# Dividing the first evacuations between VectorE and ScalarE, and moving the second key and query transposes two units later

## The chip, the cores and the metric

One Trainium2 chip; the kernel runs on 1 of its cores. A core has TensorE (matrix products and transposes, writes to PSUM), VectorE, ScalarE, GpSimd, and queues that start DMA transfers, above all that of SyncE. The metric is device time in microseconds (us) of one execution. Three executions of the kernel before took 439.0, 439.33 and 446.64 us, median 439.33.

## The reference, cut to what matters

All in float32. Attention over 512 local and 32 global positions per head (4 batches, 8 heads, width 64), then a soft mixture of experts (8 experts with 4 slots each), then a dense layer with squared ReLU:

```python
def attention(q_l, k_l, v_l, q_g, k_g, v_g):
    out_g = softmax(scale * q_g @ concat(k_g, k_l).T) @ concat(v_g, v_l)
    s_ll  = where(abs(pos[:, None] - pos[None, :]) <= 32, scale * q_l @ k_l.T, -1e9)
    out_l = softmax(concat(scale * q_l @ k_g.T, s_ll)) @ concat(v_g, v_l)
    return concat(out_g, out_l)                   # 4 x 8 x 544 x 64 -> 2304 x 512 tokens
def moe(x):                                       # soft dispatch, 8 small MLPs, soft combine
    d = softmax(x @ phi, axis=tokens); c = softmax(x @ phi, axis=slots)
    return c @ experts(d.T @ x, w1, w2)
def dense(x):
    return maximum(x @ w_in, 0) ** 2 @ w_out
```

## The kernel before, in words

Attention comes first (about the first 155 us of the span), then the experts, then the dense layer. Only the first 60 us or so matter here.

**Units.** The local positions are cut into 16 blocks of 32. A unit is one block of queries and half of the heads: `("l", s, half)` has the local queries of block s, `("g", s, half)` the global queries against the keys that lie around block s. `units` lists 44 of them; their numbers go 0, 1 = `("l",0,0)`, `("l",0,1)`; 2, 3 = `("g",0,..)`; 4, 5 = `("l",1,..)`; 6, 7 = `("l",2,..)`; 8 = `("l",3,0)` and so on. "Unit 4" below is the fifth of them.

**What one unit runs through.** TensorE computes its scores (`emit_S`, L330 or L336) into one of two PSUM buffers. VectorE scans them in four pieces (L341: scale, mask, row minimum) into one `s_buf`. GpSimd subtracts the minimum (L354) from `s_buf` into `pe_buf`. ScalarE takes the exponential (`emit_exp`, L364). TensorE transposes the result (`emit_T`, L372, two PSUM buffers `pp`), VectorE or ScalarE copies it out (`PT_BY`; L144 is VectorE, L146 ScalarE). TensorE multiplies by the values (`emit_AV`, L391), VectorE divides by the row sum (L406 to L408).

**The order is written out by hand.** In step n of the main loop stand, in this order: scores of unit n, exponential of unit n-1, the items at place 0, value products of the units that are due (two units at a time, three steps later at the earliest), the transposes of unit n-2, the items at place 1, the items at place 2, then loads (`late`). Every engine works through its instructions in that order; a wait on one holds up all behind it.

**Items.** Keys and queries arrive in pairs of blocks, positions along the partitions, and must be transposed: `item_k(i, half)` and `item_q(s, half)` each issue four TensorE transposes (L219) into one of the two buffers of `ps_tr` and four copies (eight where the two blocks don't lie in order) from there into `kT` or `qz`. `K_AT` and `Q_AT` say in which step, at which place and by which engine. `load_k`, `load_q` and `load_v` bring the next pair or block; their issues stand in one row on SyncE's queue, and each waits until the buffer it fills has been read.

**The copies out of one PSUM tile.** Where VectorE and ScalarE both read the same PSUM tile, the program makes the second engine wait for the first.

**Before the loop.** `item_k(1)` (first pair of keys): half 0 copied by VectorE, half 1 by ScalarE. `item_q(0)` the same. `global_k`: heads 0 to 3 copied by ScalarE, heads 4 to 7 by VectorE. ScalarE needs one table load (L146, ACT_TABLE_LOAD) ahead of its first activation. Unit 0 needs the first half of each, unit 1 the second.

**What the change touches.** `item_k(3, 0)` and `item_k(3, 1)` stand in steps 0 and 1, `item_k(5, 0)` in step 5 ahead of the transposes of unit 3, `item_q(2, 0)` and `item_q(2, 1)` in steps 2 and 3. Unit 4 is the first that needs the keys of `item_k(3)`, unit 6 the first that needs the queries of `item_q(2)`, unit 8 the first that needs `item_k(5)`. Values: three blocks fit beside the global ones, so `load_v(s+3)` waits until the last value product of block s is done; the first such load waits for that of unit 3 and is needed by units 4 and 5.

## Time and profile before

| | |
|---|---|
| time, median of 3 executions | 439.33 us (439.0 to 446.64) |
| the profiled execution | 439.9 us, of it span 438.1 us (first to last instruction) |
| TensorE busy | 401.0 us, 92% of the span |
| VectorE, ScalarE, GpSimd busy | 295.7, 232.4 and 132.9 us |
| first scores (unit 0) begin | 12.90 us |
| value products of units 2 and 3 end, first later value load is issued | 31.64 and 31.71 us |
| value products of units 4 and 5 begin | 37.44 us |

How to read it: the page gives busy time by engine and the chain of work that ended last. The timeline lists instructions in order of time, runs of the same kind merged, each with its start, its duration and, in brackets, the idle time of its engine before it and what ended that. PE is TensorE, DVE VectorE, ACT ScalarE, POOL GpSimd, SPq the queue of SyncE.

### The profile page before, as it was taken

To read this page: it belongs to the slowest core of one execution; us is meant where nothing else is said; L and a number is where in the kernel's file an instruction comes from. 1 tells how busy PE (TensorE), PEld (TensorE's weight loads), DVE (VectorE), ACT (ScalarE), POOL (GpSimd) and SP (SyncE) were. 2 spreads that over 40 slices of the span, in tenths; PEclk is the share of its full clock that TensorE was granted. 3 is DMA by queue.
4 is the path that set the end of the run, shared out by engine and by line. 5 is a ranking of instruction groups with operands and counts; after the bars stand their busy time and mean duration, and the time that the engine had idled before them with its cause. 6 is when DMAs were issued, how large, how long until landed. Compare 5 with 4: busy or idle time off the path is not lost.

```text
span 438.1 us, 12444 instructions
## 1 busy us (share of the span) xinstructions
PE 401.0 (92%) x4899; PEld 305.6 (70%) x4899; DVE 295.7 (67%) x951; ACT 232.4 (53%) x539; POOL 132.9 (30%) x159
## 2 busy tenths in 40 slices
PE   6788879977988987998999999999999999999993
PEld 5676767765666764354587877878877888888882
DVE  5596877765897976212599999778996555644451
ACT  3677768787465332121467666565655443444441
POOL 6244543643444431110255533234542000000000
PEclk9899999999899899999999999999999999999997
DMA  5887987899273499999913434300002400500004
GB/s 144 203 248 197 290 258 191 305 259 329 68 244 110 113 368 360 356 406 408 392 56 106 128 105 120 119 3 0 1 1 50 95 1 12 132 3 1 0 0 121
DMA packets 54938, 69.03 MB, mean 158 GB/s; under 512 B 24032, under 2 KB 40416, under 8 KB 54880
## 3 DMA queue, kind: packets, MB, share of 16 engines
q1 hardware_dynamic: 53600, 67.45, 48.6%
q10 hardware_dynamic: 1280, 0.79, 0.6%
q8 instruction: 38, 0.62, 0.6%
q14 instruction: 20, 0.16, 0.1%
HBM read 63.77 MB, written 4.46 MB: 156 GB/s over the span
## 4 chain that ended last, share of the span: by engine, by line
PE 55%; DVE 19%; DMA 10%; issue 7%; ACT 5%; POOL 1%; SPq 1%; ACTq 1%; POOLq 0%; DVEq 0%
PE ops L1118 9%; PE ops L1119 9%; PE ops L1120 9%; DMA arena_v<-in_v_l_dram 4%; PE sp L330 3%; PE xp L391 3%; PE hps L913 3%; PE ops L941 3%; DVE arena_a L543 3%; DMA arena_a<-in_moe_w_out_dram 3%; PE pp L372 3%; DVE al L1090 3%; DVE arena_b L341 2%; DMA arena_b<-in_moe_w_in_dram 2%; PE hp L1079 2%
## 5 line engine op out<-in xcount | busy, mean ns | idle before, releaser
L1118 PE MATMUL ops<-w_hl,ah 128*128 128x512 f32 x272 | 107.6, 395 | 0.0
L1119 PE MATMUL ops<-w_hl,ah 128*128 128x512 f32 x272 | 106.7, 392 | 0.4 <-POOL w_hl L860 0.4
L1120 PE MATMUL ops<-w_hl,al 128*128 128x512 f32 x272 | 106.1, 390 | 0.0
L1083 DVE TENSOR_TENSOR arena_a<-hp,arena_a 128x384 f32<-128x384 f32 x96 | 46.8, 529 | 46.1 <-ACT arena_a L1082 46.0
L1082 ACT ACTIVATE arena_a<-hp 128x384 f32<-128x384 f32 x96 | 40.2, 471 | 66.0 <-PE hp L1079 65.9
L1120 PEld LDWEIGHTS ops<-w_hl,al 128*128 128x128 f32 x272 | 51.1, 188 | 11.3 <-DVE al L1090 0.3
L354 POOL TENSOR_TENSOR arena_r<-arena_b,nm 128x512 f32<-128x512 f32 x32 | 39.7, 1241 | 62.9 <-DVE nm L341 29.3
L1089 ACT ACTIVATE ah<-arena_a 128x384 fp32r<-128x384 f32 x96 | 45.0, 505 | 25.9 <-DVE arena_a L1083 25.9
L1118 PEld LDWEIGHTS ops<-w_hl,ah 128*128 128x128 f32 x272 | 51.0, 188 | 11.0 <-issue 0.8
L1119 PEld LDWEIGHTS ops<-w_hl,ah 128*128 128x128 f32 x272 | 51.1, 188 | 10.6 <-POOL w_hl L860 1.8
L1090 DVE TENSOR_TENSOR al<-arena_a,ah 128x384 fp32r<-128x384 f32 x96 | 50.0, 561 | 8.1 <-ACT ah L1089 4.1
L146 ACT ACTIVATE arena_b<-tp 64x256 f32<-64x256 f32 (+2 forms) x135 | 43.6, 350 | 12.6 <-PE tp L219 7.8
L558 POOL TENSOR_TENSOR arena_a<-arena_a 128x512 int32<-128x512 int32 x23 | 29.7, 1293 | 51.1 <-DVE arena_a L556 48.6
L330 PE MATMUL sp<-arena_b 64*32 64x128 f32 x1024 | 37.2, 283 | 5.3 <-issue 3.2
L341 DVE CUSTOM_DVE_ANT_0 arena_b<-sp,arena_r 128x128 f32<-128x128 f32 x128 | 29.5, 286 | 16.6 <-PE sp L330 10.9
L330 PEld LDWEIGHTS sp<-arena_b 64*32 64x32 f32 x1024 | 27.5, 110 | 12.8 <-issue 9.7
L364 ACT ACTIVATE arena_r<-arena_r 128x512 f32<-128x512 f32 x44 | 27.7, 629 | 15.4 <-POOL arena_r L354 15.1
L391 PE MATMUL xp<-arena_v,arena_t 128*32 128x65 f32 x1408 | 26.5, 223 | 9.0 <-ACT arena_t L146 3.6
L391 PEld LDWEIGHTS xp<-arena_v,arena_t 128*32 128x32 f32 x1408 | 21.9, 110 | 14.5 <-issue 4.6
L372 PE MATMUL pp<-ident,arena_r 128*128 128x128 f32 x176 | 29.3, 290 | 2.4 <-ACT arena_r L364 2.3
L860 POOL TENSOR_TENSOR w_hl<-arena_a,w_hl 128x512 fp32r<-128x512 f32 x16 | 21.4, 1338 | 32.2 <-DMA arena_a<-in_moe_w_out_dram 16.3
L372 PEld LDWEIGHTS pp<-ident,arena_r 128*128 128x128 f32 x176 | 19.1, 143 | 9.9 <-issue 3.8
(188 smaller groups left out, 591.0 us busy)
## 6 DMA issues: line engine op xcount, KB each, us to landing
arena_a<-in_moe_w_dram SPq DMA_DIRECT2D x35, 512.0 KB, 6.8
arena_b<-in_moe_w_dram SPq DMA_DIRECT2D x21, 512.0 KB, 7.3
arena_a<-in_moe_w_out_dram SPq DMA_DIRECT2D x16, 512.0 KB, 5.2
arena_v<-in_v_l_dram SPq DMA_DIRECT2D x16, 256.0 KB, 4.5
arena_b<-in_moe_w_in_dram SPq DMA_DIRECT2D x8, 512.0 KB, 4.9
arena_a<-in_moe_w_in_dram SPq DMA_DIRECT2D x8, 512.0 KB, 3.9
out_dram<-arena_a SPq DMA_DIRECT2D x64, 64.0 KB, 1.7
arena_k<-in_k_l_dram SPq DMA_DIRECT2D x30, 128.0 KB, 4.0
```

Source lines behind the costliest of these rows:

```text
L146: nc.scalar.activation(out=out, in_=in_, func=AF.Copy)
L330: nc.tensor.matmul(sp[r + 32 * e:r + 32 * e + 32, j], qz[d, (s + 2) % 3, hp, b], keys, start=True, stop=True, tile_position=(64 * e, r + 3 ...
L354: nc.gpsimd.tensor_tensor(out=pe.rearrange("p j (r k) -> p j k r", k=4), in0=s_buf.rearrange("p j (k r) -> p j k r", k=4), in1=nm.unsqueez ...
L372: nc.tensor.transpose(pp[:, j], pe_buf[n % NPE][:, j], ident)
L391: nc.tensor.matmul(xp[32 * b:32 * b + 32, 2 * h + e], p, V[:, b, 4 * half + 2 * h + e], start=True, stop=True)
L1082: nc.scalar.activation(out=r[:, :N], in_=hp[:, :N], func=AF.Relu)
L1083: nc.vector.tensor_tensor(out=a[:, :N], in0=hp[:, :N], in1=r[:, :N], op=ALU.mult)
L1089: nc.scalar.activation(out=ah[:, s], in_=a, func=AF.Copy)
L1090: nc.vector.tensor_tensor(out=al[:, s], in0=a, in1=ah[:, s].bitcast(F32), op=ALU.subtract)
L1118: nc.tensor.matmul(op, ah[:, s], w_hi, start=begin, stop=False)
L1119: nc.tensor.matmul(op, ah[:, s], w_lo, start=False, stop=False)
L1120: nc.tensor.matmul(op, al[:, s], w_hi, start=False, stop=end)
```

## The change

The copies of `item_k(1)`, `item_q(0)` and `global_k` are divided within each half: of each tile VectorE copies the first part (`e` = 0, or `i` = 0) and ScalarE the second. The copies of the global keys' heads 0 to 3 come ahead of those of the second half of the queries. Both engines have as many of these copies as before, 14 each. `item_k(3)` goes from steps 0 and 1 to steps 2 and 3, `item_q(2)` from steps 2 and 3 to steps 4 and 5, `item_k(5, 0)` from place 0 to place 2 of step 5, the loads that follow them likewise. The loads of the first two blocks of values and of the global values stand ahead of `load_q(2)` on SyncE's queue, and those of two of the four batches of global keys ahead of SyncE's part of `load_q(0)`.

```diff
@@ -221,11 +221,14 @@
 
     def global_k(kg_sb):
         tp = transpose4(kg_sb, ps_x, "x")
-        for n in range(2):
+
+        def evac_half(n):
             h = slice(2 * n, 2 * n + 2)
             for i in range(2):
                 evac(kT[:, h].rearrange("p h b s q -> p (h b) s q")[:, :, 6 + i, :],
-                     tp[:, h].rearrange("p h (b q) -> p (h b) q", b=B), 1 - n)
+                     tp[:, h].rearrange("p h (b q) -> p (h b) q", b=B), i)
+
+        return evac_half
 
     def global_q(qg_sb):
         tp = transpose4(qg_sb, ps_m, "m")
@@ -234,10 +237,12 @@
             evac(qgz.rearrange("p h b e q -> p (h b) e q")[s, :, e, :],
                  tp[s].rearrange("p h (b q) -> p (h b) q", b=B), e)
 
-    def item_k(i, half, who=1):
+    def item_k(i, half, who=1, other=None):
         tp = transpose_pairs(k_buf, half)
         p0, p1 = POS[i % 6], POS[(i + 1) % 6]
         for e in range(2):
+            if e and other is not None:
+                who = other
             for r in range(2):
                 src = tp[64 * r:64 * r + 64, e].rearrange("p h (b k q) -> p (h b) k q", b=B, k=2)
                 dst = kT[64 * e:64 * e + 64, 2 * half:2 * half + 2].rearrange("p h b s (q r) -> p (h b) s q r", r=2)[..., r]
@@ -247,11 +252,13 @@
                     evac(dst[:, :, p0, :], src[:, :, 0, :], who)
                     evac(dst[:, :, p1, :], src[:, :, 1, :], who)
 
-    def item_q(s, half, who=1, *where):
+    def item_q(s, half, who=1, *where, other=None):
         tp = transpose_pairs(q_buf, half, *where)
         z = qz[:, :, 2 * half:2 * half + 2].rearrange("p s h b (q r) -> p s (h b) q r", r=2)
         s0, s1 = (s + 2) % 3, s % 3
         for e in range(2):
+            if e and other is not None:
+                who = other
             for r in range(2):
                 src = tp[64 * r:64 * r + 64, e].rearrange("p h (b s q) -> p s (h b) q", s=2, q=16)
                 dst = z[64 * e:64 * e + 64, :, :, :, r]
@@ -289,11 +296,11 @@
     XT_BY = (0, 0, 0, 0, 0, 1, 0, 0, 0, 1, 0, 1, 0, 1, 1, 1)
 
     K_AT = {
-        1: (0, 0, 1), 2: (0, 2, 1), 3: (-1, 2, 1), 4: (0, 0, 1), 5: (-1, 2, 1), 6: (0, 2, 1), 7: (0, 2, 1),
+        1: (0, 2, 1), 2: (0, 2, 1), 3: (-1, 2, 1), 4: (0, 0, 1), 5: (-1, 2, 1), 6: (0, 2, 1), 7: (0, 2, 1),
         8: (0, 0, 1), 9: (-1, 2, 1), 10: (-1, 0, 1), 11: (0, 0, 0), 12: (-1, 2, 1),
     }
     Q_AT = {
-        0: (1, 1, 0), 1: (-1, 1, 0), 2: (0, 2, 1), 3: (0, 2, 1), 4: (-1, 0, 1), 5: (0, 1, 1), 6: (0, 0, 1),
+        0: (3, 1, 0), 1: (1, 1, 0), 2: (0, 2, 1), 3: (0, 2, 1), 4: (-1, 0, 1), 5: (0, 1, 1), 6: (0, 0, 1),
         7: (0, 2, 1), 8: (0, 0, 1), 9: (0, 2, 1), 10: (0, 1, 0), 11: (0, 0, 1), 12: (-1, 2, 1), 13: (0, 0, 0),
     }
 
@@ -620,10 +627,16 @@
         nc.vector.tensor_copy(out=perm.rearrange("p (b q) -> p b q", b=B), in_=ident.rearrange("p (q b) -> p b q", b=B))
         idle_products(7, ps_s, "s", ident)
         kg_sb, qg_sb = x_buf[0], x_buf[1]
+
+        def load_kg(b):
+            nc.sync.dma_start(out=kg_sb[32 * b:32 * b + 32], in_=k_g[b].rearrange("h q d -> q h d"))
+
         load_k(1)
+        load_kg(0)
+        load_kg(1)
         load_q(0)
-        for b in range(B):
-            nc.sync.dma_start(out=kg_sb[32 * b:32 * b + 32], in_=k_g[b].rearrange("h q d -> q h d"))
+        load_kg(2)
+        load_kg(3)
         for b in range(B):
             nc.sync.dma_start(out=qg_sb[32 * b:32 * b + 32], in_=q_g[b].rearrange("h q d -> q h d"))
         nc.vector.memset(V[:, :, :, D:VW], 1.0)
@@ -654,13 +667,13 @@
                 d, pos, who = Q_AT[s]
                 at(l0 if s % 2 else l1, pos, item_q, s + 1 if s % 2 else s + 2, s % 2, who, d=d)
             if s % 2 and s + 3 < NJ:
-                after(l0, load_q, s + 3)
+                after(l0 if s > 1 else l1, load_q, s + 3)
             if s % 2 == 0 and 0 < s <= NJ - 6:
                 after(l0, load_k, s + 5)
             at(l1, X_AT[s], emit_xT, s, d=av_at(index[l1]) - index[l1] + 1)
-        at(("l", 0, 0), 0, item_k, 3, 0, 1)
-        at(("l", 0, 1), 0, item_k, 3, 1, 1)
-        after(("l", 0, 1), load_k, 5)
+        at(("g", 0, 0), 0, item_k, 3, 0, 1)
+        at(("g", 0, 1), 0, item_k, 3, 1, 1)
+        after(("g", 0, 1), load_k, 5)
         for i in range(NM - 1):
             l1 = ("l", NT * i + NT - 1, 1)
             d = av_at(index[l1]) - index[l1]
@@ -696,10 +709,12 @@
                 fn(*args)
 
         for half in range(2):
-            item_k(1, half, half)
-        for half in range(2):
-            item_q(0, half, half, ps_pt, "pt")
-        global_k(kg_sb)
+            item_k(1, half, 0, other=1)
+        item_q(0, 0, 0, ps_pt, "pt", other=1)
+        evac_gk = global_k(kg_sb)
+        evac_gk(0)
+        item_q(0, 1, 0, ps_pt, "pt", other=1)
+        evac_gk(1)
 
         def load_vg():
             nc.sync.dma_start(out=V[3:128:4, :, :, 0:D].rearrange("p b h d -> p (b h) d"),
@@ -709,10 +724,10 @@
             nc.sync.dma_start(out=phi_sb, in_=phi.rearrange("(c p) s -> p c s", p=128))
 
         load_k(3)
-        load_q(2)
         load_v(1)
         load_v(2)
         load_vg()
+        load_q(2)
         late.setdefault(3, []).append((win_load, (0,)))
         late.setdefault(5, []).insert(0, (load_phi, ()))
         for n in range(NU + LA):
```

The program's order on ScalarE up to the last copy of the global keys (tp_193 and tp_202 are the halves of the first keys; tp_211 and tp_224, with the change tp_211 and tp_231, those of the queries; tp_237, with the change tp_224, the global keys), before, with the semaphores that each instruction waits for:

```order
L146 ACT_TABLE_LOAD
L146 ACTIVATE arena_b_91<-tp_202 64x8x2x16 [waits PE_49]
L146 ACTIVATE arena_b_91<-tp_202 64x8x2x16 x3
L146 ACTIVATE arena_b_91<-tp_224 64x128 [waits PE_49]
L146 ACTIVATE arena_b_91<-tp_224 64x128 x7
L146 ACTIVATE arena_b_91<-tp_237 128x8x32 [waits PE_49]
L146 ACTIVATE arena_b_91<-tp_237 128x8x32
```

and with the change:

```order
L146 ACT_TABLE_LOAD [waits DVE_49]
L146 ACTIVATE arena_b_91<-tp_193 64x8x2x16 [waits PE_49]
L146 ACTIVATE arena_b_91<-tp_193 64x8x2x16
L146 ACTIVATE arena_b_91<-tp_202 64x8x2x16 [waits DVE_49,PE_49]
L146 ACTIVATE arena_b_91<-tp_202 64x8x2x16
L146 ACTIVATE arena_b_91<-tp_211 64x128 [waits DVE_49,PE_49]
L146 ACTIVATE arena_b_91<-tp_211 64x128 x3
L146 ACTIVATE arena_b_91<-tp_224 128x8x32 [waits DVE_49]
L146 ACTIVATE arena_b_91<-tp_231 64x128 [waits DVE_49,PE_49]
L146 ACTIVATE arena_b_91<-tp_231 64x128 x3
L146 ACTIVATE arena_b_91<-tp_224 128x8x32 [waits DVE_49]
```

The first activation now reads a tile that VectorE reads first. Its wait for VectorE stands ahead of the table load, where before the table load waited for nothing.

ScalarE from there to the copy of the transposed exponentials of unit 1 (arena_r is `pe_buf`, pp the transposed tile, the tiles tp_287, tp_320, tp_336 and tp_376 those of `item_k(3)`), before:

```order
L146 ACTIVATE arena_b_91<-tp_287 64x8x2x16 [waits PE_49]
L146 ACTIVATE arena_b_91<-tp_287 64x8x2x16 x3
L364 ACTIVATE arena_r_99<-arena_r_99 128x512 [waits Pool_49]
L146 ACTIVATE arena_b_91<-tp_320 64x8x2x16 [waits PE_49]
L146 ACTIVATE arena_b_91<-tp_320 64x8x2x16 x3
L364 ACTIVATE arena_r_99<-arena_r_99 128x512 [waits Pool_49]
L146 ACTIVATE arena_t_79<-pp_358 128x512 [waits PE_49]
L364 ACTIVATE arena_r_99<-arena_r_99 128x512 [waits Pool_49]
L146 ACTIVATE arena_t_79<-pp_398 128x512 [waits PE_49]
```

and with the change:

```order
L371 ACTIVATE arena_r_99<-arena_r_99 128x512 [waits Pool_49] x2
L146 ACTIVATE arena_b_91<-tp_336 64x8x2x16 [waits PE_49]
L146 ACTIVATE arena_b_91<-tp_336 64x8x2x16 x3
L146 ACTIVATE arena_t_79<-pp_345 128x512 [waits PE_49]
L371 ACTIVATE arena_r_99<-arena_r_99 128x512 [waits Pool_49]
L146 ACTIVATE arena_b_91<-tp_376 64x8x2x16 [waits PE_49]
L146 ACTIVATE arena_b_91<-tp_376 64x8x2x16 x3
L146 ACTIVATE arena_t_79<-pp_385 128x512 [waits PE_49]
```

The copies of `item_k(3)` stood ahead of the exponentials of units 0 and 1; now they stand behind both, and ahead of the copies of the transposed tiles (arena_t) of units 0 and 1.

TensorE from the value products of units 0 and 1 to those of units 2 and 3 (sp are scores, xp value products, arena_k and arena_q the sources of the items' transposes), before:

```order
L391 MATMUL xp_438<-arena_v_95,arena_t_79 32x65 x16
L391 MATMUL xp_459<-arena_v_95,arena_t_79 32x65 x16
L372 MATMUL pp_480<-ident_64,arena_r_99 128x128 x4
L330 MATMUL sp_493<-arena_b_91 32x128 x16
L219 MATMUL tp_517<-arena_b_91,arena_k_83 128x128 x4
L372 MATMUL pp_530<-ident_64,arena_r_99 128x128 x4
L212 MATMUL tp_536<-ident_64,arena_a_75 128x128 x4
L330 MATMUL sp_546<-arena_b_91 32x128 x16
L391 MATMUL xp_570<-arena_v_95,arena_t_79 32x65 x16
L391 MATMUL xp_588<-arena_v_95,arena_t_79 32x65 x16
```

and with the change:

```order
L398 MATMUL xp_420<-arena_v_95,arena_t_79 32x65 x16
L398 MATMUL xp_441<-arena_v_95,arena_t_79 32x65 x16
L379 MATMUL pp_462<-ident_64,arena_r_99 128x128 x4
L219 MATMUL tp_468<-arena_b_91,arena_q_87 128x128 x4
L337 MATMUL sp_480<-arena_b_91 32x128 x16
L379 MATMUL pp_504<-ident_64,arena_r_99 128x128 x4
L219 MATMUL tp_510<-arena_b_91,arena_q_87 128x128 x4
L212 MATMUL tp_519<-ident_64,arena_a_75 128x128 x4
L219 MATMUL tp_525<-arena_b_91,arena_k_83 128x128 x4
L337 MATMUL sp_546<-arena_b_91 32x128 x16
L398 MATMUL xp_570<-arena_v_95,arena_t_79 32x65 x16
L398 MATMUL xp_588<-arena_v_95,arena_t_79 32x65 x16
```

Both halves of `item_q(2)` have come in (tp_468, tp_510), and `item_k(5, 0)` (tp_525) stands directly ahead of the scores of unit 6. `ps_tr` has two buffers, so tp_525 takes the one that tp_510 leaves, once VectorE has copied it. On VectorE the copies of tp_468 and one step of the w_in conversion (L553) stand ahead of the scans of unit 5, those of tp_510 directly behind them.

## Rows read from the trace of the kernel before

**Rows 1.** Page, part 5: xcount | busy us, mean ns | idle before.

```profile
L341 DVE CUSTOM_DVE_ANT_0 arena_b<-sp,arena_r 128x128 f32<-128x128 f32 x128 | 29.5, 286 | 16.6 <-PE sp L330 10.9
```

**Rows 2.** Stretches: length, busy us of PE, PEld, DVE, ACT, POOL; clock, DMA, GB/s.

```profile
12.90:23.60 10.70, 10.42 (x188) 8.29 (x188) 6.79 (x39) 6.79 (x14) 3.40 (x3) 0.84 0.84 204
23.60:31.70 8.10, 6.99 (x214) 5.42 (x210) 7.80 (x39) 5.39 (x15) 3.55 (x3) 1.00 0.89 261
...
160.00:180.00 20.00, 17.17 (x230) 8.69 (x234) 11.54 (x43) 3.66 (x16) 3.03 (x13) 1.00 0.94 338
```

**Rows 3.** Chain of waits, 33 to 46 us: start, us, what.

```profile
33.66 1.42 issue
...
37.51 1.08 PE xp L391 x64
...
38.65 5.74 DMA arena_v<-in_v_l_dram
...
44.52 1.14 PE xp L391 x64
```

**Rows 4.** Timeline to the first scores: start, us, engine, instruction, idle before.

```profile
3.74 1.28 ACT L146 ACT_TABLE_LOAD   x1 [3.74 <-issue]
...
7.52 1.73 DVE L144 COPY arena_b<-tp 64x256 f32<-64x256 f32 x4 [2.49 <-PE tp L219]
...
8.37 1.62 ACT L146 ACTIVATE arena_b<-tp 64x256 f32<-64x256 f32 x4 [3.35 <-PE tp L219]
...
8.73 1.61 PE L219 MATMUL tp<-arena_b,arena_q 128*128 128x128 f32 x8 [0.40 <-DMA arena_q<-in_q_l_dram]
...
10.38 2.47 ACT L146 ACTIVATE arena_b<-tp 64x128 f32<-64x128 f32 x10 [0.39 <-PE tp L219]
...
12.90 1.62 PE L330 MATMUL sp<-arena_b 64*32 64x128 f32 x32 [2.12 <-ACT arena_b L146]
```

**Rows 5.** Timeline, units 0 and 1, same columns.

```profile
15.36 1.06 PE L219 MATMUL tp<-arena_b,arena_k 128*128 128x128 f32 x4
...
18.60 0.63 ACT L364 ACTIVATE arena_r<-arena_r 128x512 f32<-128x512 f32 x1
...
18.76 1.14 POOL L354 TENSOR_TENSOR arena_r<-arena_b,nm 128x512 f32<-128x512 f32 x1 [1.87 <-DVE nm L341]
...
19.25 1.65 ACT L146 ACTIVATE arena_b<-tp 64x256 f32<-64x256 f32 x4
...
22.86 0.58 ACT L146 ACTIVATE arena_t<-pp 128x512 f32<-128x512 f32 x1
```

**Rows 6.** Timeline, units 2 to 6, same columns.

```profile
20.97 1.78 DVE L144 COPY arena_b<-tp 64x256 f32<-64x256 f32 x4
...
23.64 1.15 PE L391 MATMUL xp<-arena_v,arena_t 128*32 128x65 f32 x64
...
25.31 1.08 PE L330 MATMUL sp<-arena_b 64*32 64x128 f32 x32
...
25.68 0.29 DVE L341 CUSTOM_DVE_ANT_0 arena_b<-sp,arena_r 128x128 f32<-128x128 f32 x1
...
26.31 0.66 PE L219 MATMUL tp<-arena_b,arena_k 128*128 128x128 f32 x4
...
28.02 0.42 DVE L553 TENSOR_SCALAR arena_b<-arena_b 128x512 int32<-128x512 uint32 x1
...
30.97 0.67 PE L391 MATMUL xp<-arena_v,arena_t 128*32 128x65 f32 x32 [0.76 <-ACT arena_t L146]
```

**Rows 7.** Timeline, SyncE's queue: the key load behind item_k(3).

```profile
18.18 2.92 SPq L161 DMA_DIRECT2D arena_k<-in_k_l_dram  x4
```

**Rows 8.** DMA issues: KB, us to landing; w_in, values, global keys (4).

```profile
arena_b<-in_moe_w_in_dram SPq DMA_DIRECT2D x1, 512.0 KB, 4.7
...
arena_v<-in_v_l_dram SPq DMA_DIRECT2D x1, 256.0 KB, 5.1
...
DMA to landing us min/median/max: 3.1/3.9/4.8
```

## The prediction

> **What bounds the kernel now.** I read the stretches of busy time first, then the chain of waits in order of time, then the timeline of the first 45 us, because everything that the change touches lies there. The reader is to see three things. First, nothing is full in the beginning: the first scores start at 12.90 us, and TensorE had stood idle for 2.12 us, waiting for ScalarE's last copy [rows 4]. Second, between 23.60 and 31.70 us VectorE is the fullest engine, 7.80 of 8.10 us [rows 2]. Third, from there the chain runs through the values: the value products of units 4 and 5 start at 37.51, as soon as they are over the next block of values is requested (38.65), it lands 5.74 us later, and the products of units 6 and 7 start at 44.52, right behind it [rows 3]. So what counts for the end is not when the first scores start but when the products of unit 3 are done (30.97 + 0.67 = 31.64 [rows 6]), since the first later block of values is requested then and takes 5.1 us [rows 8]: it lands at 36.8, 0.7 before its use at 37.51. A delay beyond this 0.7 goes into the loads of values behind it.
>
> **The change, part by part.** The times of the kernel with the change that follow are estimates, from durations in the rows and the order in which the instructions now stand.
>
> *Division of the first copies.* The count is the same, 14 copies on each engine. Before, ScalarE loads its table at 3.74 for 1.28 us, in idle time, and starts copying at 8.37 [rows 4]. Now its wait for VectorE stands ahead of the table load. VectorE starts at 7.52 and needs 1.73 / 4 = 0.43 us a copy [rows 4], so two are done at 8.4. Then ScalarE loads until 9.7, copies four key pieces (1.62, to 11.4), four query pieces and one of the global keys. The 2.47 us for eight of the small kind and two of the large [rows 4] give 0.90 for the four and 0.33 for the one: 12.6. The first scores start at about 12.65 instead of 12.90. What the division gains, some 1.5 us, the table load takes back but for 0.25.
>
> *Loads in the beginning.* Two loads of global keys now stand ahead of two of the queries. The queries had landed when TensorE took them at 8.73, after a wait of 0.40 [rows 4]. What the queries lose is bounded by nothing from below and by the spread of the four loads of global keys from above (3.1 to 4.8 us to landing, so 1.7 [rows 8]). Without delay VectorE has copied its part of the first query half at 10.6, and ScalarE, with the keys until 11.4, hides 0.8 of it; the far end would leave 0.9. I take 0, which is nearer to a load of only 128 KB more in front. The values sooner on SyncE's queue are worth nothing: the first value products start at 23.64 behind TensorE's own work, with no wait for a transfer [rows 6]. `load_q(2)` behind them has until 26 us.
>
> *Second keys two units later.* Their transposes, 1.06 us [rows 5], and their copies no longer stand between the scores of units 0 and 1. With the 0.25 above, unit 1 is scanned about 1.1 us sooner, and GpSimd's subtraction for unit 1 ends at 18.8 instead of 18.76 + 1.14 = 19.9 [rows 5]. GpSimd reads the only `s_buf`, so the scans of units 2 and 3 come sooner as well, and without the query copies between them (1.78 us [rows 6]) unit 4 is scanned at 23.6 instead of 25.68 [rows 6].
>
> But ScalarE has the key copies behind both exponentials now. From 18.8 on it must do, in this order and without a pause: exponential 0.63, key copies 1.65, copy of the transposed unit 0 0.6, exponential 0.63, key copies 1.65, copy of unit 1 0.58 [rows 5]. That is 5.74, with the gaps between them 5.85: the copy for unit 1 is done at about 24.65, where it was done at 22.86 + 0.58 = 23.44 [rows 5]. The value products of unit 1 wait for it until 24.7; they end near 25.3 instead of 23.64 + 1.15 = 24.8 [rows 6]. All of TensorE's work stands behind them. So this part, 1.1 us ahead at first, is 0.5 us behind here.
>
> *Second queries two units later.* Behind these products TensorE transposes unit 2 and the first half of the queries, 0.6 each, to 26.4. VectorE then copies it (1.78), does a step of the w_in conversion (0.42 [rows 6]), scans unit 5 (4 x 29.5 / 128 = 0.9 [rows 1]) and copies the second half (1.78): 31.4. Only then is the PSUM buffer free for the transposes of `item_k(5, 0)`. Those take 0.66, the scores of unit 6 1.08, the products of units 2 and 3 1.15 [rows 6]: 34.2 to 34.5. Before, it was 31.64. The difference is 2.6 to 2.9; the 0.7 of slack leaves 1.9 to 2.2.
>
> *The loads that follow.* `load_k(5)` follows the moved transposes, 2.6 us later than at 18.18, and takes SyncE 2.92 us as before [rows 7]; the w_in block behind it is issued near 23.6 and lands 4.7 us later [rows 8], at 28.3, when VectorE asks for it: hidden, or 0.3 late. The load of `load_q(4)` now stands right ahead of the values that count, but is issued by 31.4.
>
> *Sum.* 1.9 to 2.2 us by the slack, up to 0.3 more for w_in: +2.2. Two things can move it. TensorE stood still for 1.42 us at 33.66 with no releaser in the profile [rows 3]; if that stop comes again behind the later scores of unit 7, the products of unit 4 start at 40.5 and not 39.7, +3.0. And in 12.90 to 23.60 the granted clock was 0.84 [rows 2], full speed and for a while half (1.2 instead of 2.4 GHz); without that drop the start would be some 0.5 to 1.3 us sooner, which leaves +0.9. The profiled execution took 439.9, so it would take 442.1; it stands 0.57 above the median of 439.33. Against the median: **441.5 us**, own range 440.2 to 442.4.
>
> **Rivals.**
>
> *The table load costs twice.* The trace shows the table load itself as 1.28 us [rows 4], and no instruction close behind it, so a further stop after it would not be seen in it. The Trainium skill (ScalarE: Activation LUTs, section "What ACT_TABLE_LOAD costs") puts a DRAIN of about 1.38 us beside a load of about 1.28, some 2.66 together; the load agrees with the trace, the drain no run here shows yet. As a mechanism of this kernel: if ScalarE stands still after the load for as long as the load takes, the first scores start at 13.9, the subtraction for unit 1 ends at 20.1 instead of 18.8, and all that follows comes 1.3 later: 442.8. Chance 0.08.
>
> *The delay is taken up.* Between 160 and 180 us DMA is busy 0.94 [rows 2]. If the weights for the experts come no later because attention runs later, the time is that of before, 439 to 440. For it: that share. Against it: the buffers into which these weights go come free only when attention is over. Chance 0.22.
>
> *The first gain is kept.* Unit 4 is scanned 2.1 us sooner (23.6 against 25.68 [rows 6]). If VectorE is the bound, as its 7.80 of 8.10 us say [rows 2], and the values are not, this gain goes through: 437.2. The point from which it decides: the products of unit 3 must end by 31.6 or sooner, so that the copies of the second queries and the transposes of `item_k(5, 0)` cannot follow one after the other as above. Against it: the order leaves no other way for the one PSUM buffer. Chance 0.26.
>
> *No difference in the order.* That the change doesn't do what it says is out: the order shows the moves.
>
> **How the numbers follow.** Forecast (slower by 0.9 to 3.1) 0.44, first gain kept 0.26, delay taken up 0.22, table load twice 0.08. The range leaves out the far end of the gain (sooner than 437.0, about 0.1) and of the delays (later than 443.2, about 0.08): 437.0 to 443.2. A difference of 2% is 8.8 us, about what a measurement of this kernel can tell from no change; none of the cases comes near it. For what none of them names I leave 0.02 on the fast side and 0.03 on the slow side: faster 0.02, within 2% 0.95, slower 0.03.
>
> **What the profile of the changed kernel would show.** Right: the table load near 8.4 and not 3.7; first scores near 12.65; the subtraction for unit 1 ending near 18.8; ScalarE without a pause from there to 24.65; the transposes of `item_k(5, 0)` near 31.5, waiting for VectorE; the value load behind unit 3 issued at 34.2 or later; the products of unit 4 near 39.7. Wrong: the table load early, or unit 3's products over before 32 us. The forecast as a whole is wrong if the products of unit 4 start 2 us later and the kernel still ends no later, or if unit 4 starts before 37.5.

## The result and the profile after

The kernel with the change takes 441.75 us, median of 22 executions (436.34 to 449.59). The kernel before was run as often beside it and has a median of 437.2 us (432.94 to 446.64). The ratio is **1.0078, 95% interval 1.0049 to 1.0107**: 3.4 us slower (2.1 to 4.7). The forecast of 441.5 us names the time to 0.3 us, but partly by luck: it stood on a median of 439.33 us from three executions and added 2.2 us, while 3.4 us were lost. A second set of the change, below, lost more (1.017), so the size of the loss is known only roughly. Ratios here and below compare undisturbed executions of both kernels, and the two profiled ones (443.9 us, span 442.1, of the change; 439.9 us, span 438.1, of before) are not among these.

**To the first scores** ([rows 4]): timeline of the kernel after, columns as there.

```profile
6.13 1.06 PE L219 MATMUL tp<-arena_b,arena_k 128*128 128x128 f32 x8 [1.43 <-DMA arena_k<-in_k_l_dram]
...
7.74 1.28 ACT L146 ACT_TABLE_LOAD   x1 [7.74 <-DVE arena_b L144]
9.03 1.62 ACT L146 ACTIVATE arena_b<-tp 64x256 f32<-64x256 f32 x4
9.04 1.08 PE L219 MATMUL tp<-arena_b,arena_q 128*128 128x128 f32 x4 [1.84 <-DMA arena_q<-in_q_l_dram]
...
10.16 1.45 DVE L144 COPY arena_b<-tp 64x128 f32<-64x128 f32 x5 [1.62 <-PE tp L219]
...
11.25 1.31 ACT L146 ACTIVATE arena_b<-tp 64x128 f32<-64x128 f32 x5 [0.60 <-DVE arena_b L144]
...
12.61 1.08 PE L337 MATMUL sp<-arena_b 64*32 64x128 f32 x32 [0.78 <-ACT arena_b L146]
```

The table load has moved from 3.74 to 7.74, and its releaser is VectorE. The first scores start at 12.61 (forecast 12.65). But ScalarE, which the forecast has working without a pause, waited 0.60 us at 11.25 for VectorE's query copies; these waited for TensorE, and TensorE had waited 1.84 us for the queries, where it waited 0.40 before. It took them only 0.31 us later than before (9.04 and 8.73); the wait is longer because the key transposes were over at 7.19 (6.13 + 1.06) instead of 8.33, as this line of before has it:

```profile
6.39 1.94 PE L219 MATMUL tp<-arena_b,arena_k 128*128 128x128 f32 x8 [1.70 <-DMA arena_k<-in_k_l_dram]
```

In this execution the table load was covered, and the queries set the time.

**Units 0 to 3** ([rows 5 to 7]): same view.

```profile
17.12 1.13 POOL L361 TENSOR_TENSOR arena_r<-arena_b,nm 128x512 f32<-128x512 f32 x1 [1.05 <-DVE nm L348]
18.28 0.63 ACT L371 ACTIVATE arena_r<-arena_r 128x512 f32<-128x512 f32 x1 [1.54 <-POOL arena_r L361]
...
18.94 1.64 ACT L146 ACTIVATE arena_b<-tp 64x256 f32<-64x256 f32 x4
...
21.62 1.61 ACT L146 ACTIVATE arena_b<-tp 64x256 f32<-64x256 f32 x4
...
23.26 0.60 ACT L146 ACTIVATE arena_t<-pp 128x512 f32<-128x512 f32 x1
...
23.91 0.67 PE L398 MATMUL xp<-arena_v,arena_t 128*32 128x65 f32 x32 [1.60 <-ACT arena_t L146]
...
25.64 1.79 DVE L144 COPY arena_b<-tp 64x256 f32<-64x256 f32 x4
...
28.07 0.43 DVE L560 TENSOR_SCALAR arena_b<-arena_b 128x512 int32<-128x512 uint32 x1 [0.65 <-DMA arena_b<-in_moe_w_in_dram]
...
29.36 1.78 DVE L144 COPY arena_b<-tp 64x256 f32<-64x256 f32 x4
...
31.24 0.63 PE L219 MATMUL tp<-arena_b,arena_k 128*128 128x128 f32 x4 [3.05 <-issue]
...
33.10 1.96 PE L398 MATMUL xp<-arena_v,arena_t 128*32 128x65 f32 x64
...
35.13 0.60 SPq L173 DMA_DIRECT2D arena_v<-in_v_l_dram  x1
```

This is the chain of the forecast, step by step: the subtraction for unit 1 ends at 18.25 instead of 19.9, ScalarE then has no pause until 23.86, unit 1's products wait 1.60 for it, VectorE copies the second queries from 25.64 to 27.43 and from 29.36 to 31.14, and only at 31.24 do the transposes of `item_k(5, 0)` run, behind a stop of 3.05 us. The profile names no releaser ("issue"); what ended right before is VectorE's copy. Unit 3's products end at 35.06, where they ended at 31.64.

The granted clock of stretches of the kernel after (length, busy us by engine, clock, DMA, GB/s):

```profile
11.96:32.45 20.49, 14.85 (x324) 11.54 (x328) 13.94 (x73) 11.81 (x30) 6.75 (x6) 1.00 0.76 190
32.45:35.86 3.41, 3.41 (x84) 2.85 (x77) 1.27 (x9) 2.66 (x9) 1.17 (x1) 0.50 0.74 261
...
169.00:179.20 10.20, 9.40 (x52) 4.11 (x48) 6.27 (x23) 0.93 (x4) 1.20 (x4) 0.50 0.70 278
```

1.2 us behind the end of the stop TensorE falls to 1.2 GHz for 3.41 us and is busy all of it. The products that took 1.15 us before take 1.96. The chain of waits ([rows 3]) goes on:

```profile
31.24 0.63 PE tp L219 x4
31.87 1.30 PE sp L337 x32
33.17 1.89 PE xp L398 x64
...
39.53 1.07 PE xp L398 x64
...
40.66 6.37 DMA arena_v<-in_v_l_dram
...
47.16 1.13 PE xp L398 x64
```

Units 4 and 5 come at 39.53 instead of 37.51, and TensorE works up to them without a wait for the values: the block issued at 35.13 landed 3.5 us later, where the one of before took 5.1. The next block takes 6.37 us instead of 5.74, and units 6 and 7 come at 47.16, 2.64 later than before.

When each later value load is issued (L173 on SyncE's queue, us from the start), in these two traces and in three of the experiments:

| | 1st | 2nd | 3rd | 4th | 5th | 6th | 7th | 8th | 9th | 10th | 11th | 12th | 13th | 14th |
|---|---|---|---|---|---|---|---|---|---|---|---|---|---|---|
| before | 31.7 | 38.6 | 45.7 | 56.5 | 65.0 | 72.0 | 83.8 | 91.3 | 98.0 | 115.8 | 122.3 | 129.2 | 142.4 | 149.8 |
| after | 35.1 | 40.7 | 48.3 | 58.4 | 67.9 | 74.6 | 86.5 | 94.3 | 101.3 | 115.8 | 121.8 | 131.7 | 144.0 | 150.1 |
| before again | 32.7 | 38.7 | 45.3 | 56.5 | 64.3 | 71.2 | 83.3 | 91.7 | 98.4 | 114.1 | 120.5 | 127.8 | 140.3 | 147.8 |
| value load later | 36.0 | 42.5 | 49.7 | 60.9 | 68.8 | 75.8 | 88.2 | 96.0 | 101.7 | 115.6 | 122.1 | 128.9 | 142.1 | 148.1 |
| division alone, table early | 31.1 | 37.1 | 43.8 | 54.8 | 64.5 | 71.1 | 82.7 | 90.7 | 97.9 | 112.2 | 118.1 | 125.1 | 138.3 | 144.3 |

Up to the ninth load the change is 1.9 to 3.4 us behind the first trace of before. At the tenth it is level: the trace of before has a stretch of half clock at 108.8 and another at 143.0, that of after at 93.9 and 128.0. The last load is 0.2 us late, and nearly all of the 4.0 us by which the two spans differ arises behind it, where the trace of the change has 10.24 us of half clock at 169. Against the second trace of before the change is 1.7 us late at the tenth load and 2.3 at the last. So this pair of traces shows how the delay arises, but not that it lasts. For that the experiments are needed.

The table shows a second loss. Between the 11th and the 12th load 10.0 us pass in the change, 6.9 and 7.2 in the traces of before. After, then before:

```profile
125.70 0.66 ACT L547 ACTIVATE arena_b<-arena_b 128x512 f32<-128x512 f32 x1 [4.53 <-DMA arena_b<-in_moe_w_in_dram]
...
126.94 0.66 PE L379 MATMUL pp<-ident,arena_r 128*128 128x128 f32 x4 [3.02 <-ACT arena_r L371]
```

```profile
124.69 0.67 ACT L540 ACTIVATE arena_b<-arena_b 128x512 f32<-128x512 f32 x1 [2.98 <-DMA arena_b<-in_moe_w_in_dram]
...
125.93 0.66 PE L372 MATMUL pp<-ident,arena_r 128*128 128x128 f32 x4 [1.50 <-ACT arena_r L364]
```

ScalarE must first convert a block of w_in that has not landed, and the exponential for which TensorE waits stands behind it. In seven of the fourteen traces (both of the change, moves alone, queries alone, both with the other PSUM pair, and the one with late second queries) this stop is 2.4 to 3.2 us long, half clock follows it or has already begun, and 9.3 to 10.2 us lie between the two loads; in the other seven the stop is 1.0 to 1.6 us long, there is no half clock, and 6.4 to 7.2 us lie between the loads. No experiment follows this up.

### The profile page after: what moved, and what is told of

It reads as the page before. It is cut to its first block, busy times and chain, and to the rows that moved or that the text cites. A ratio compares the mean times of both kernels' runs of the same rounds, so it can differ in the third digit from the quotient of the medians.

```text
span 442.1 us, 12447 instructions
## 1 busy us (share of the span) xinstructions
PE 404.5 (91%) x4899; PEld 307.7 (70%) x4899; DVE 294.8 (67%) x951; ACT 232.6 (53%) x539; POOL 132.6 (30%) x159
## 4 chain that ended last, share of the span: by engine, by line
PE 56%; DVE 14%; DMA 11%; ACT 7%; issue 6%; POOL 2%; SPq 2%; POOLq 0%; DVEq 0%; ACTq 0%
PE ops L1133 10%; PE ops L1134 9%; PE ops L1135 9%; DMA arena_a<-in_moe_w_out_dram 4%; PE sp L337 4%; PE hps L928 4%; PE xp L398 3%; PE ops L956 3%; PE pp L379 3%; ACT arena_b L146 3%; DMA arena_v<-in_v_l_dram 3%; PE hp L1094 2%; DMA arena_b<-in_moe_w_in_dram 2%; DVE arena_a L550 2%; DVE arena_a L563 2%
## 5 line engine op out<-in xcount | busy, mean ns | idle before, releaser
L146 ACT ACTIVATE arena_b<-tp 64x256 f32<-64x256 f32 (+1 forms) x135 | 43.6, 349 | 7.4 <-PE tp L219 4.1
L337 PE MATMUL sp<-arena_b 64*32 64x128 f32 x1024 | 36.3, 278 | 0.9 <-ACT arena_b L146 0.8
L398 PE MATMUL xp<-arena_v,arena_t 128*32 128x65 f32 x1408 | 28.3, 231 | 8.9 <-ACT arena_t L146 3.4
L398 PEld LDWEIGHTS xp<-arena_v,arena_t 128*32 128x32 f32 x1408 | 23.4, 116 | 14.9 <-issue 4.4
## 6 DMA issues: line engine op xcount, KB each, us to landing
arena_k<-in_k_l_dram SPq DMA_DIRECT2D x30, 128.0 KB, 4.0
```

The costliest lines, as they stand in the source:

```text
L146: nc.scalar.activation(out=out, in_=in_, func=AF.Copy)
L337: nc.tensor.matmul(sp[r + 32 * e:r + 32 * e + 32, j], qz[d, (s + 2) % 3, hp, b], keys, start=True, stop=True, tile_position=(64 * e, r + 3 ...
L398: nc.tensor.matmul(xp[32 * b:32 * b + 32, 2 * h + e], p, V[:, b, 4 * half + 2 * h + e], start=True, stop=True)
```

## The experiments

### Which part costs: division, moves, keys, queries

**Division alone** (the change with its moves undone, its load order kept):

```diff
 K_AT
-        1: (0, 2, 1),
+        1: (0, 0, 1),
 Q_AT
-        0: (3, 1, 0), 1: (1, 1, 0),
+        0: (1, 1, 0), 1: (-1, 1, 0),
...
-                after(l0 if s > 1 else l1, load_q, s + 3)
+                after(l0, load_q, s + 3)
...
-        at(("g", 0, 0), 0, item_k, 3, 0, 1)
-        at(("g", 0, 1), 0, item_k, 3, 1, 1)
-        after(("g", 0, 1), load_k, 5)
+        at(("l", 0, 0), 0, item_k, 3, 0, 1)
+        at(("l", 0, 1), 0, item_k, 3, 1, 1)
+        after(("l", 0, 1), load_k, 5)
```

> The change without its moves: the first copies divided, two loads of global keys and the value loads sooner, but the second key and query transposes where they stood before. Theory (the moves cost the time, the division costs nothing): first scores at 12.5 to 12.7 us, product of unit 3 over by 31.6, second value load requested near 38.7, ratio to the kernel before 0.998 to 1.001. Rival (the division, with the table load behind the wait for VectorE, costs the time): ratio 1.004 or more, as with the whole change, although the value products of units 4 and 5 are on time. A third outcome, the first scores 0.3 us sooner and this carried through, would be 0.999, which is not to be told from the theory.

Measured: ratio 1.0043 (0.997 to 1.0116), which holds both answers. In the trace the first scores start at 12.77, unit 3's products end at 32.19 (0.6 later than expected), units 4 and 5 start at 36.94, 0.5 sooner than in the first trace of before. Not settled by its time; by the trace the products of units 4 and 5 were on time.

**Moves alone** (the kernel before with the other side of that diff, loads and copies as before):

> The moves without the division: the first copies by whole halves as before, loads in the order of before, but the second key and query transposes two units later. Theory (the moves cost the time): first scores at 12.9 us, VectorE copies both halves of the queries between 25 and 31.5, the transposes of item_k(5, 0) at 31 to 32, value products of units 4 and 5 at 39 to 40, ratio to the kernel before 1.005 to 1.009. Rival (the division costs it): ratio 0.999 to 1.002, unit 4's products near 37.5.

Measured: ratio **1.0174 (1.0117 to 1.023)**, medians 442.29 and 436.98. First scores 12.84, and the same stop:

```profile
31.78 0.63 PE L219 MATMUL tp<-arena_b,arena_k 128*128 128x128 f32 x4 [2.43 <-issue]
...
33.35 1.13 PE L391 MATMUL xp<-arena_v,arena_t 128*32 128x65 f32 x64
...
39.84 1.13 PE L391 MATMUL xp<-arena_v,arena_t 128*32 128x65 f32 x64 [0.90 <-ACT arena_b L146]
```

The moves cost the time, more than the 1.005 to 1.009 expected, and more than the whole change in its first set (the intervals do not meet); sizes from different sets can therefore not be subtracted from each other. In this trace no half clock follows the stop, and units 4 and 5 wait for ScalarE and for the values, which landed 5.2 us after their issue at 34.55, until the same moment.

**The two moves apart**, each on the kernel before; queries (with the place of `item_k(5, 0)` and `load_q(4)`):

```diff
-        1: (0, 0, 1),
+        1: (0, 2, 1),
-        0: (1, 1, 0), 1: (-1, 1, 0),
+        0: (3, 1, 0), 1: (1, 1, 0),
-                after(l0, load_q, s + 3)
+                after(l0 if s > 1 else l1, load_q, s + 3)
```

> The kernel before with item_q(2) alone moved two steps later (with load_q(4) behind it and item_k(5, 0) at place 2 of step 5); the keys of item_k(3) stay where they were. By the prediction this is the larger part: transposes of item_k(5, 0) wait for VectorE's copy of the second half, unit 3's products end at 33.5 to 34.5 us instead of 31.6, units 4 and 5 start at 38.5 to 40, ratio 1.003 to 1.008. Rival (the keys behind both exponentials, which hold up ScalarE, are what costs): unit 3's products end before 32.2, ratio 0.998 to 1.002.

and keys:

```diff
-        at(("l", 0, 0), 0, item_k, 3, 0, 1)
-        at(("l", 0, 1), 0, item_k, 3, 1, 1)
-        after(("l", 0, 1), load_k, 5)
+        at(("g", 0, 0), 0, item_k, 3, 0, 1)
+        at(("g", 0, 1), 0, item_k, 3, 1, 1)
+        after(("g", 0, 1), load_k, 5)
```

> The kernel before with item_k(3) alone moved two steps later (with load_k(5) behind it); the queries of item_q(2) stay. By the prediction this is the smaller part, ScalarE's chain of two exponentials, two key copies and two copies of transposed tiles: unit 1's products end 0.5 us later than before, unit 3's products at 31.8 to 32.6, units 4 and 5 at 37.5 to 38.2, ratio 0.999 to 1.003. Rival (this is the larger part): unit 3's products after 33.5, ratio 1.004 or more.

Measured: queries 1.0108 (1.0041 to 1.0174), keys 1.005 (1.0007 to 1.0094). The trace of the queries alone, then of the keys alone:

```profile
32.38 1.09 PE L219 MATMUL tp<-arena_b,arena_k 128*128 128x128 f32 x4 [2.43 <-issue]
35.26 1.96 PE L391 MATMUL xp<-arena_v,arena_t 128*32 128x65 f32 x64
...
41.50 1.14 PE L391 MATMUL xp<-arena_v,arena_t 128*32 128x65 f32 x64
```

```profile
27.93 0.63 PE L219 MATMUL tp<-arena_b,arena_k 128*128 128x128 f32 x4 [1.56 <-DMA arena_k<-in_k_l_dram]
...
32.73 0.67 PE L391 MATMUL xp<-arena_v,arena_t 128*32 128x65 f32 x32 [1.69 <-ACT arena_t L146]
...
37.64 1.14 PE L391 MATMUL xp<-arena_v,arena_t 128*32 128x65 f32 x64 [0.17 <-DMA arena_v<-in_v_l_dram]
```

The queries are the larger part: unit 3's products end at 37.22 (half clock from 31.0 for 6.83 us), 2.7 us past the far end of what was expected, and units 4 and 5 come 4.1 us late. The keys alone end unit 3's products at 33.40, beyond the expected 32.6, by a wait not foreseen: their load moves with them, and `item_k(5, 0)` at its old place waits 1.56 for it. But the value load had nearly that much slack, since it landed 4.0 us after its issue: units 4 and 5 are 0.2 late against the first trace of before (1.0 against the second, below). The ratios agree in order; their intervals overlap.

### The first scores: table load or queries

**The change with its table loaded early:**

```diff
         load_q(0)
+        nc.scalar.activation(out=slots[:, 0, 0:1], in_=ident[:, 0:1], func=AF.Copy)
         load_kg(2)
```

> The whole change, and one tiny ScalarE activation ahead of the first copies (one column of the identity into the column of slots that the kernel writes later), so that the table is loaded in idle time, near 3.7 us. The prediction's own step (the table load takes back 1.2 us of the division's gain): first scores near 11.4 us, ScalarE's first key copies at about 7.7. Theory from the trace of the change (ScalarE waits for VectorE's query copies anyway, TensorE for the queries): first scores at 12.3 to 12.6. Time: equal to the whole change within 0.002 by both, since the later copies of the queries bind.

Measured: ratio 1.0131 (1.0066 to 1.0196), not clear of the change's 1.0078. Table load at 3.74, key copies from 8.31, then

```profile
9.29 1.09 PE L219 MATMUL tp<-arena_b,arena_q 128*128 128x128 f32 x4 [1.11 <-DMA arena_q<-in_q_l_dram]
...
11.50 1.30 ACT L146 ACTIVATE arena_b<-tp 64x128 f32<-64x128 f32 x5 [1.50 <-DVE arena_b L144]
...
12.85 1.93 PE L337 MATMUL sp<-arena_b 64*32 64x128 f32 x32 [0.77 <-ACT arena_b L146]
```

The early load buys nothing: ScalarE only waits longer, 1.50 instead of 0.60, and the first scores come even a little later than expected, with the queries. That the table load alone holds them back, which would give 11.4 here, is refuted.

**Division without moves, table early, queries ahead of all global keys:**

```diff
         load_k(1)
-        load_kg(0)
-        load_kg(1)
         load_q(0)
+        load_kg(0)
+        load_kg(1)
         load_kg(2)
         load_kg(3)
+        nc.scalar.activation(out=slots[:, 0, 0:1], in_=ident[:, 0:1], func=AF.Copy)
```

> The division without the moves, with the queries loaded ahead of all global keys as before the change, and one tiny ScalarE activation ahead of the first copies, so that the table is loaded near 3.7 us. Theory (with the division the queries' landing sets the first scores, and TensorE's pause for them keeps it at half clock): queries transposed right behind the keys at 8.3 to 8.8, the 64x128 score products of unit 0 from 11.2 to 11.9 us, ratio to the kernel before 0.994 to 1.000. Rival (the copies themselves or the clock set the first scores): first scores at 12.4 or later, ratio as for e1_divide_only.

Measured: ratio 1.0009 (0.9959 to 1.0058). First scores at 12.10, later than 11.2 to 11.9: the query transposes came at 8.53 without a wait, but the first four took 1.09 us, where the next four took 0.60. With both limits gone, 0.8 us are gained on the kernel before. They are lost again at 21.48, where the loads of values stand ahead of `load_q(2)` and the second queries, not moved here, are late:

```profile
21.48 1.08 PE L219 MATMUL tp<-arena_b,arena_q 128*128 128x128 f32 x4 [2.89 <-DMA arena_q<-in_q_l_dram]
```

**The same with `load_q(2)` ahead of the values, as before the change:**

```diff
         load_k(3)
+        load_q(2)
         load_v(1)
         load_v(2)
         load_vg()
-        load_q(2)
```

> The division alone, in the load order of the kernel before (queries ahead of all global keys, second queries ahead of the values), with the table loaded early and no moves: the version that by the experiments so far has only the gain of the division. Theory: first scores at 11.9 to 12.2 us (12.10 with this start in e7_divide_queries_first) instead of 12.90, no wait for the second queries, unit 3's products over by 30.8 to 31.6, ratio 0.996 to 1.000. Rival (nothing of the beginning's gain reaches the values): unit 3's products at 31.6 or later, ratio 1.000 to 1.002.

Measured: ratio 0.994 (0.989 to 0.999), medians 437.52 and 440.08. First scores at 12.19, unit 3's products over at 31.01, units 4 and 5 at 35.95. **The kernel before once more**, beside it on the chip:

> The kernel before once more, unaltered, as a measure of what two sets of runs of one kernel differ by, and for a second trace of it: ratio 0.997 to 1.003. The stretches of half clock (at 13.3, 108.8 and 143.0 us in the first trace) fall elsewhere if they belong to the execution and not to the kernel; the products of unit 3 should be over near 31.6 and units 4 and 5 start near 37.5 again.

Measured: ratio 0.9959 (0.9898 to 1.002), median 440.35. Unit 3's products end at 32.62, 1.0 us later than in the first trace, and units 4 and 5 start at 36.61, 0.8 sooner; differences of this size between two traces are not an effect of an edit. Half clock stands at 14.2 and 140.5 us, near two of the three places of the first trace; that at 108.8 does not come again. Two sets of one kernel can thus differ by 0.4%, and the version with the division alone is not shown to be faster than before: it is 2.6 to 2.8 us below both medians, and in the table its value loads are between 0.2 us behind and 3.5 us ahead of the second trace of before. Shown is that the division, with loads and table in the right place, costs nothing.

### The stop: buffer, queue or transfers

**The change, the second half of `item_q(2)` transposed into the other PSUM pair**, so that `item_k(5, 0)` needs not wait for VectorE:

```diff
-                at(l0 if s % 2 else l1, pos, item_q, ..., s % 2, who, d=d)
+                at(l0 if s % 2 else l1, pos, item_q, ..., s % 2, who, *((ps_pt, "pt") if s == 1 else ()), d=d)
```

> The whole change, but the second half of the queries of item_q(2) is transposed into the other PSUM pair (ps_pt), so that item_k(5, 0) needs not wait until VectorE has copied it out. TensorE's order stays that of the change. Theory (the wait for this one buffer is the step that costs the time): transposes of item_k(5, 0) near 28.2 us instead of 31.2, product of unit 3 over by 31.5 to 33, units 4 and 5 at 37.5 to 38.2, ratio to the kernel before 0.999 to 1.003. Rival (ScalarE's chain behind both exponentials, or the late w_in block, costs the time): value products of units 4 and 5 still after 39, ratio 1.006 or more.

Measured: ratio 1.0184 (1.0136 to 1.0233), medians 443.44 and 436.98.

```profile
29.54 0.60 PE L219 MATMUL tp<-arena_b,arena_k 128*128 128x128 f32 x4
30.07 1.08 PE L337 MATMUL sp<-arena_b 64*32 64x128 f32 x32
31.07 1.13 PE L398 MATMUL xp<-arena_v,arena_t 128*32 128x65 f32 x64
...
39.35 1.14 PE L398 MATMUL xp<-arena_v,arena_t 128*32 128x65 f32 x64 [2.63 <-DMA arena_v<-in_v_l_dram]
```

```profile
29.29 3.04 SPq L161 DMA_DIRECT2D arena_q<-in_q_l_dram  x4
32.37 1.07 SPq L603 DMA_DIRECT2D arena_a<-in_moe_w_dram  x2
33.54 0.60 SPq L173 DMA_DIRECT2D arena_v<-in_v_l_dram  x1
```

The stop is gone and unit 3's products end at 32.20, as expected. But `load_q(4)`, which moved with the queries, and two loads of weights behind it hold SyncE's queue until 33.5, and the values come at 39.35: a stop of 2.63 in place of the one removed (no half clock follows it). So the numbers of the rival came true, though not by the waits it named. The theory as stated, that the wait for the buffer is the cost, fails: it is only the first of several limits.

**The same, the two loads of weights behind the value load:**

```diff
     PIECES = (
-        0, 0, 0, 0, 1, 2, 0, 0, 1, 1, 1, 1, ...
+        0, 0, 0, 0, 1, 0, 2, 0, 1, 1, 1, 1, ...
```

> The kernel of e4_q2h1_pt, with the two loads of expert weights that stood ahead of the first later value load on SyncE's queue put behind it. In e4 unit 3's products were over at 32.2 us, but the value load was issued only at 33.54, behind load_q(4) and these two, and landed at 39.3. Theory (with the PSUM buffer free, SyncE's queue is what is late next): value load issued at 32.3 to 32.6, landing 5.1 to 5.8 later, products of units 4 and 5 at 37.4 to 38.4, the weights 2 us later at no cost, ratio to the kernel before 1.000 to 1.004. Rival (the landing time is set by how much the other loads move, not by the order of issue): units 4 and 5 still after 39.

Measured: ratio 1.0158 (1.0094 to 1.0222), medians 445.68 and 439.02, on a second chip.

```profile
35.23 0.67 PE L398 MATMUL xp<-arena_v,arena_t 128*32 128x65 f32 x32 [0.17 <-DMA arena_v<-in_v_l_dram]
...
44.27 1.57 PE L398 MATMUL xp<-arena_v,arena_t 128*32 128x65 f32 x64 [2.64 <-DMA arena_v<-in_v_l_dram]
```

The value load is issued at 30.75 and units 4 and 5 start at 35.23, 2.2 us sooner than before. The next value load, issued at 37.15 behind the weights, lets units 6 and 7 start at 44.27, as before the change, behind a stop of 2.64. "At no cost" was wrong. With the stop gone and units 4 and 5 ahead of before, the kernel is still as slow as the change itself on that chip (1.017, below): nothing of the loss is shown to come back. Why it ends 1.6% later though level with the one before at 44 us is open; its trace has half clock at 44.8, 92.6, 126.7 and 143.8, and 10.0 us between the 11th and the 12th value load, as the change has.

### Does a delay of the values reach the end?

The kernel before, the first later value load behind the key load of its step:

```diff
             late.setdefault(av_at(last_of(s)), []).insert(0, (load_v, (s + 3,)))
+        late[6].insert(1, late[6].pop(0))
```

> The kernel before with one thing altered: the first later value load stands behind the key load of the same step on SyncE's queue, and is issued near 35.4 instead of 31.7 us. No engine's order changes. Theory (a delay of this load beyond its 0.7 us of slack goes through to the end): products of units 4 and 5 at 39.5 to 40.6, ratio 1.004 to 1.008. Rival (the delay is taken up later, where the weights are awaited): units 4 and 5 as late, but ratio 0.998 to 1.002.

Measured: ratio **1.0065 (1.002 to 1.0109)**, 2.9 us (0.9 to 4.8) on a median of 439.02.

```profile
35.95 0.61 SPq L173 DMA_DIRECT2D arena_v<-in_v_l_dram  x1
```

```profile
41.30 1.14 PE L391 MATMUL xp<-arena_v,arena_t 128*32 128x65 f32 x64 [4.21 <-DMA arena_v<-in_v_l_dram]
```

```profile
37.10:41.30 4.20, 0.00 (x0) 0.03 (x1) 1.17 (x9) 1.30 (x3) 2.85 (x3) 1.00 0.73 214
42.38:45.79 3.41, 3.41 (x44) 3.02 (x40) 1.80 (x6) 1.34 (x4) 0.00 (x0) 0.50 0.38 81
```

No engine's order differs, units 4 and 5 are 3.9 us late, and by the ratio about 2.9 of it arrives at the end: the delay is not taken up in full. The trace does not show where it goes through: against the second trace of before the value loads are 3.3 us late at the ninth, 1.6 at the tenth and 0.3 at the last, and the span is 436.1 us. Again a stop (4.21 us) is followed by half clock, 1.1 us behind its end.

### The change a second time

> The change once more, unaltered, for a second trace of it. The first trace had the granted clock at half from 32.5 to 35.9 and from 169 to 179 us. If these stretches belong to the kernel, they are there again; if they fall anywhere, this trace has them elsewhere. The steps of the trace should repeat: transposes of item_k(5, 0) at 31 to 33, products of units 4 and 5 at 39 to 40.5. Ratio 1.005 to 1.012.

Measured, on the second chip (as were the value load made later and the division with the queries ahead): ratio 1.017 (1.0109 to 1.0232), medians 446.88 and 439.02. That is more than expected, and its interval lies above that of the first set. Part of it is clock: the mean granted clock was 0.967 here and 0.977 in the first set, and over the executions of before beside the three sets of experiments 0.01 less goes with 2.7 to 3.8 us more. Why the clock was lower is not known. The steps repeat: transposes of `item_k(5, 0)` at 32.57 behind a stop of 3.03 us, units 4 and 5 at 41.99, beyond the expected 40.5, since the half clock began at 31.77, in the stop, and lasted 6.83 us. Near 170 it lasts 3.41 us here (from 171.7), not 10.24.

### Stops and half clock, over all fourteen traces

Stops of TensorE behind the first 17 us, and how many were followed by half clock (the granted clock falls between the stop's begin and 2 us after its end):

| stop of TensorE | number | followed by half clock |
|---|---|---|
| 1.3 to 1.8 us | 31 | 2 |
| 1.8 to 2.35 us | 15 | 8 |
| 2.35 us or more | 27 | 21 |

Between 18 and 50 us nine of the traces have a stop of 2.4 to 4.2 us: both of the change, moves alone, queries alone, the change with an early table, both versions with the other PSUM pair, the value load made later, and the one in which the second queries came late. Six of the nine have half clock in or behind it. The two traces of before, the division alone, the keys alone and the version with early table and loads as before have no stop longer than 1.8 us there, and no half clock. This was read from traces, not tested by an experiment of its own: stop and work differ together, and many of the stops are one place of the program in several traces.

## Why the prediction was right, and where it was not

**Division.** 12.65 was forecast (the terms given add up to 12.5), 12.61 measured, but by two deviations that cancel. The table load began at 7.74, not 8.4, because the first key transposes were over 1.1 us sooner. And the term set to nothing, "what the queries lose" (0 of 0 to 0.9), was mis-sized: ScalarE waited 0.60 us for their copies. In the trace with the weights behind the value load the queries came without a wait, ScalarE copied from 9.43 (behind the table load) to 13.70 without a pause, and the first scores started at 12.41: the forecast's own chain. So two limits stand close together, and loading the table early removes only one. On value loads "worth nothing" the forecast holds because the queries moved too: without that TensorE waited 0.30 us for the second queries in the division alone, and 2.89 us where the start was soonest.

**Second keys.** Subtraction for unit 1 over at 18.25 (forecast 18.8), ScalarE without a pause to 23.86 (24.65), unit 1's products over at 24.58 (25.3). All is 0.5 to 0.8 us earlier, the first keys having been transposed at 6.13 instead of 6.39 and the clock being full from 11.96. The forecast had named this case: without the drop of the clock in 12.90 to 23.60 it left +0.9 us. In the profiled execution that drop was not there, and the gain was lost again behind the stop. The chain is right; of the 0.5 us the keys alone leave 0.2 at units 4 and 5.

**Second queries.** Copies until 31.14 (31.4), transposes of `item_k(5, 0)` at 31.24 (31.5), unit 3's products over at 35.06 (34.2 to 34.5), w_in 0.65 late for VectorE (up to 0.3), units 4 and 5 at 39.53 (39.7). The step that failed in size is the one from the transposes to the products: it was priced at full clock (0.66 + 1.08 + 1.15), and took 3.82 us, since the stop brought half clock behind it. The forecast looked at the clock only in 12.90 to 23.60. The Trainium skill (TensorE: Matmul & The Clock Gate, section "HAM oscillation — how this bites in real kernels") tells of a TensorE that idles for a transfer and works at half rate behind it. The traces agree where the value load was made later (4.21 us of stop, then the clock at 0.50 for 3.41), and for a wait on a copied PSUM buffer too: 3.05 us of stop, then the clock at 0.50 for 3.41. That forecast and measurement still meet at units 4 and 5 is because the slow work took the place of the wait for the values, which landed in 3.5 us and not in 5.1: two terms missed by about 0.9 and 1.6 us in opposite directions.

**The sum.** 2.2 us forecast, 3.4 measured (2.1 to 4.7). The half clock, which costs up to 1.7 us (half of 3.41) where TensorE is busy throughout, is of the size that lacks, but it is not shown to be what lacks: in two traces with the same stop and no half clock behind it (moves alone, early table) units 4 and 5 start at 39.84 and 40.50, no sooner than in the change. Nor is it shown that the 2.0 us at units 4 and 5 are the ones lost at the end: with the other PSUM pair and the value load first these units start 2.2 us sooner than before, and the loss stays. What is shown is that the moves cost time, the queries alone at least 0.4%; on which way it reaches the end the agreement of the sum says nothing.

**The rivals.** *Table load twice*: the first ACTIVATE starts at 9.03, where the load ends (7.74 + 1.28 = 9.02). There is no further stop, and the drain that the Trainium skill (ScalarE: Activation LUTs, section "What ACT_TABLE_LOAD costs") puts beside the load is not seen here. *Delay taken up*: against it the value load made later: of 3.9 us some 2.9 are there at the end by the ratio, 0.9 at the least; some may be taken up. The forecast's own argument against it does not hold for all weights: loads of expert weights stand on SyncE's queue from 24 us on. *First gain kept*: unit 4 was scanned at 23.10, sooner even than forecast, but unit 3's products ended 3.5 us past the point that was to decide, 31.6.

**What stays open.** Near 170 us, half clock of 10 us or more stands in five traces (after, moves alone, early table, other PSUM pair, keys alone), behind no long stop; it is in neither trace of before, but nor in that of the queries alone or the second of the change. Whether the change brings it about is not known; in the pair of profiled executions most of the difference of 4.0 us arises there. Open too is how the moved queries lead to the long stop near 125 us, which is in six of the seven traces with them and in one of the seven without.

## What to carry to other kernels

Before an item is moved in an order written by hand, follow its buffer, its own load and what stands behind that load on the queue: here three limits stood one behind the other (PSUM buffer, SyncE's queue, landing of the values), and removing the first showed the second. Removing two of them won no time back, so a limit that is gone from a trace is not yet a gain: the time has to show it. A copy that is divided between two engines pays only as far as its data and the second engine's table are there in time. And behind a stop of TensorE the work may run at the slower clock; the range of a forecast has to allow for it.

## What the runs showed of the hardware

Stops of 1.3 to 1.8 us left the clock alone in 29 of 31 cases, those of 2.35 us or more did so in 6 of 27; the half clock was 3.41 us long in most cases, 6.83 to 13.65 in some. A value load of 256 KB landed 3.5 us after its issue (the change, 35.13), 4.0 (keys alone, 33.47), 5.1 (before, 31.71), 6.4 (the change, 40.66) and 7.0 (other PSUM pair with the value load first, 37.15). The block of w_in near 120 us (512 KB) took 4.8 to 6.1 us in the seven traces with the long stop behind it, 4.3 to 4.9 in the others. The kernel before had medians of 436.98 and 440.08 us at two times on one chip and 439.02 on another, so differences of a few us are to be read only within one set.
